# Weight preparation moved from GpSimd to VectorE, and three reorderings, in a retention and two-layer feed-forward kernel

## The chip, the cores and the metric

The kernel runs on one core of a Trainium2 chip. The metric is the device time of one execution in microseconds (us). A core has TensorE (PE, with its weight loads shown as PEld), VectorE (DVE), ScalarE (ACT), GpSimd (POOL) and SyncE (SP, which here issues nearly all DMAs). Each engine runs its own instructions in the order in which they were written; semaphores tie the engines together. Times and rows below come from one profiled execution of the kernel before the change.

## The reference

Inputs are float32. There are 4 batches, 8 heads, 576 positions and a head width of 64, so 2304 tokens of 512 features.

```
scores = (q @ k.T) / sqrt(64)
ret    = scores * gamma_h ** (i - j) for i >= j, else 0
x      = (ret @ v), heads side by side            # 2304 x 512
h = x @ w_in;   g = relu(h) ** 2;              x = g @ w_out     # 512 -> 2048 -> 512
h = x @ w_in2;  g = h * clip(h + 3, 0, 6) / 6; out = g @ w_out2  # 512 -> 2048 -> 512
```

The four weight matrices arrive as 64-bit words and are decoded on the chip to float32.

## The kernel before, in words

Matmuls take float32 operands as a rounded high part and a low part (the rest), and each product is three matmuls: high by high, high by low, low by high (`PASSES`). So every operand has to be split: ACT copies the high part, DVE or POOL subtracts it to get the low part (`split_to`, lines 198 to 206).

The program has three stages. (1) Retention, and the first token block of layer one, up to about 204 us. (2) The rest of layer one, in 48 steps for token blocks of 512 (`units` i = 16 to 63; line 1119). In step i, PE does 12 matmuls for one 128-wide chunk of `h` (line 448) and 12 for the output of the chunk two steps earlier (line 506). ACT then does relu, square and the high copy of g, and the high part of the input weights of step i+2; DVE does the low part of g (line 477) and of those weights (line 201, `win`). (3) Layer two, in three token ranges (`SECOND`). It uses a seven-product scheme for 2 x 2 blocks, in both its matrix products. Each range has a *hidden* part (line 723, 8 pairs of products of `w_in2`) and a *visible* part (line 891: products P1, P2, P6, P5, P7, P3, P4 in `ORDER`, 6 steps each, 12 matmuls in a step).

**Weight preparation for layer two** goes on beside stage 2. `ready_steps` (line 539) makes, for each of 8 pairs of chunks, a list of small jobs with costs. Four are decodes (`dec`: two ACT and four DVE instructions, lines 174 to 194, and one DMA that loads a later weight chunk). One is `sums` (block sums of `w_in2`), with four splits; one is `out_sums` (the same for `w_out2`), with four `out_split`s. Stage 2 hands the jobs out in the 34 steps of `READY` (i = 17 to 58 without the last three and the first of each 16). Each such step earns `pace`, the sum of all costs over 34, and a job is issued once more than half of its cost is owed (lines 1162 to 1167). The costs of a pair sum to 176, so a pair takes 4.25 steps. A split writes a `ready` tile. There are three of these in turn (`bounce`), each is stored to DRAM by a DMA that SP issues (`keep`, line 431, and `keep_right`, line 535), and the store is written only with the next job (`store_late`). A tile is written again only once the store of three splits ago has landed; ACT's high copy is the instruction that waits for that.

**The visible part.** Step s splits the left operand of step s+2 into `gop` tiles: ACT's high copy, then DVE's low part (`split_operand`, line 829). The buffers take turns by three, so ACT's copy waits until PE has done step s-1. For the first `LONE` products these tiles lie in w0 to w2, later in the space of `plain`. After the multiplications of some steps DVE does the block sums of the last three pairs (`sum_up`, line 744), named in the table that `hidden` returns (line 800). The operands of the next range (`operand_items`) and its first weight tiles (`load_left`) are spread over the steps by the table at lines 1202 to 1207. Right operands come by DMA (`load_right`). The first `LONE` x 4 of them, and the four behind, go through four `wo` buffers and are asked for four ahead. Later ones use seven buffers, asked for seven ahead (`ask`, line 899).

**Between stages 2 and 3** the operands of the first range are made (`operand_steps`, line 603), in the order of `PRODUCTS`; the hidden part uses them as P1, P5, P6, P2, P3, P7, (P4).

## Time and profile before

| | |
|---|---|
| median of 3 runs | 856.66 us (856.44 to 857.41) |
| the profiled execution | 856.49 us, of which the span from first to last instruction is 854.7 us |
| PE busy | 823.9 us, 96% |
| PEld busy | 740.2 us, 87% |
| DVE busy | 609.9 us, 71% |
| ACT busy | 495.1 us, 58% |
| POOL busy | 144.4 us, 17% |

PE is busy nearly all the time, but its busy time counts a slowed matmul like any other, so a stage is better judged by comparing the starts of equal groups of matmuls. POOL's work ends with stage 2: after 485 us it does nothing. Up to step i = 17 (about 197 us) the change touches nothing.

### The profile page before, as it was taken

To read this page: it belongs to the slowest core of one execution; us is meant where nothing else is said; L and a number is where in the kernel's file an instruction comes from. 1 tells how busy PE (TensorE), PEld (TensorE's weight loads), DVE (VectorE), ACT (ScalarE), POOL (GpSimd) and SP (SyncE) were. 2 spreads that over 40 slices of the span, in tenths; PEclk is the share of its full clock that TensorE was granted. 3 is DMA by queue.
4 is the path that set the end of the run, shared out by engine and by line. 5 is a ranking of instruction groups with operands and counts; after the bars stand their busy time and mean duration, and the time that the engine had idled before them with its cause. 6 is when DMAs were issued, how large, how long until landed. Compare 5 with 4: busy or idle time off the path is not lost.

```text
span 854.7 us, 14951 instructions
## 1 busy us (share of the span) xinstructions
PE 823.9 (96%) x5580; PEld 740.2 (87%) x5580; DVE 609.9 (71%) x941; ACT 495.1 (58%) x894; POOL 144.4 (17%) x122
## 2 busy tenths in 40 slices
PE   8999999999999999899998999999999999999998
PEld 7888888888777787678876799999999999999998
DVE  5888777786788597794877567687477877476744
ACT  1248676776557676486766444556445455444443
POOL 2362232322344031330421000000000000000000
PEclk9999999999999999999999999999999999999999
DMA  9993665665778768865869477689376697576793
GB/s 361 350 307 125 175 193 179 194 198 196 276 252 290 242 210 300 299 221 188 300 230 330 162 249 255 186 319 402 125 254 230 189 396 283 189 252 201 222 315 122
DMA packets 80609, 208.74 MB, mean 244 GB/s; under 512 B 7958, under 2 KB 29078, under 8 KB 80536
## 3 DMA queue, kind: packets, MB, share of 16 engines
q1 hardware_dynamic: 80244, 207.52, 70.9%
q8 instruction: 44, 0.72, 0.3%
q10 hardware_dynamic: 292, 0.27, 0.1%
q14 instruction: 29, 0.24, 0.1%
HBM read 165.29 MB, written 42.47 MB: 243 GB/s over the span
## 4 chain that ended last, share of the span: by engine, by line
PE 64%; DVE 11%; DMA 10%; ACT 7%; issue 4%; POOL 3%; SPq 1%; ACTq 0%; DVEq 0%; POOLq 0%
PE hps L723 20%; PE yps L891 16%; PE hps L448 12%; PE yps L506 11%; DMA kept<-ready 4%; PE ytail L506 2%; DVE sums L677 2%; DMA stage<-in_w_in_dram 2%; DMA kvt<-in_kv_dram 1%; DVE gop L201 1%; DVE a L188 1%; DVE win L201 1%; ACT r L473 1%; POOL ready L201 1%; DVE g L477 1%
## 5 line engine op out<-in xcount | busy, mean ns | idle before, releaser
L506 PE MATMUL yps<-g,wo 128*128 128x512 f32 x768 | 194.2, 392 | 0.9 <-POOL wo L201 0.9
L448 PE MATMUL hps<-xring,win 128*128 128x512 f32 (+1 forms) x720 | 159.9, 369 | 9.6 <-ACT win L200 5.2
L506 PEld LDWEIGHTS yps<-g,wo 128*128 128x128 f32 x768 | 140.1, 188 | 29.2 <-POOL wo L201 4.1
L448 PEld LDWEIGHTS hps<-xring,win 128*128 128x128 f32 x720 | 124.2, 192 | 36.6 <-DVE win L201 8.6
L891 PE MATMUL yps<-wo,gop 128*128 128x256 f32 x1080 | 134.8, 284 | 3.8 <-DVE gop L201 3.6
L891 PEld LDWEIGHTS yps<-wo,gop 128*128 128x128 f32 x1080 | 131.4, 192 | 6.5 <-DVE gop L201 6.1
L723 PE MATMUL hps<-xlast,win 128*128 128x384 f32 x576 | 108.4, 334 | 0.7 <-DVE xlast L644 0.5
L723 PEld LDWEIGHTS hps<-xlast,win 128*128 128x128 f32 x576 | 100.4, 188 | 1.3 <-DVE xlast L644 0.8
L723 PE MATMUL hps<-xop,win 128*128 128x384 f32 x432 | 82.8, 334 | 0.4 <-ACT xall L766 0.4
L477 DVE TENSOR_TENSOR g<-r,g 128x512 fp32r<-128x512 f32 x64 | 51.0, 797 | 43.9 <-ACT g L474 42.7
L723 PEld LDWEIGHTS hps<-xop,win 128*128 128x128 f32 x432 | 75.5, 188 | 0.8 <-ACT xall L766 0.7
L448 PE MATMUL hps<-xown,win 128*128 128x512 f32 x240 | 62.0, 395 | 6.3 <-DVE win L201 3.5
L470 ACT ACTIVATE r<-hps 128x512 f32<-128x512 f32 x80 | 43.4, 542 | 34.4 <-PE hps L448 34.0
L448 PEld LDWEIGHTS hps<-xown,win 128*128 128x128 f32 x240 | 44.1, 188 | 19.1 <-DVE win L201 6.4
L736 ACT ACTIVATE v<-mixed,half_one 128x768 f32<-128x768 f32 x21 | 19.7, 938 | 61.9 <-DVE mixed L674 61.9
L200 ACT ACTIVATE gop<-sums 128x512 fp32r<-128x512 f32 x54 | 33.4, 629 | 37.8 <-PE yps L891 30.7
L200 ACT ACTIVATE win<-w 128x512 fp32r<-128x512 f32 x64 | 39.7, 620 | 25.3 <-DVE w L194 25.3
L891 PE MATMUL yps<-gop 128*128 128x256 f32 x432 | 53.6, 283 | 0.5 <-ACT xall L944 0.5
L188 DVE SCALAR_TENSOR_TENSOR a<-stage,a 128x512 int32<-128x512 int32 x64 | 51.9, 811 | 1.8
L891 PEld LDWEIGHTS yps<-gop 128*128 128x128 f32 x432 | 52.5, 192 | 0.7 <-ACT xall L944 0.7
L201 DVE TENSOR_TENSOR gop<-sums,gop 128x512 fp32r<-128x512 f32 x54 | 36.4, 689 | 22.3 <-ACT gop L200 22.3
L179 DVE TENSOR_SCALAR a<-a 128x512 f32<-128x512 f32 x64 | 35.6, 557 | 22.5 <-ACT a L175 22.5
(120 smaller groups left out, 1188.6 us busy)
## 6 DMA issues: line engine op xcount, KB each, us to landing
win<-kept SPq DMA_DIRECT2D x72, 512.0 KB
wo<-rights SPq DMA_DIRECT2D x60, 512.0 KB
wo<-kept SPq DMA_DIRECT2D x48, 512.0 KB
stage<-in_w_out_dram SPq DMA_DIRECT2D x32, 512.0 KB
kept<-ready SPq DMA_DIRECT2D x24, 512.0 KB
rights<-ready SPq DMA_DIRECT2D x24, 512.0 KB
gop<-rights SPq DMA_DIRECT2D x24, 512.0 KB
kept<-wo SPq DMA_DIRECT2D x16, 512.0 KB
```

The source lines that it names most:

```text
L179: nc.vector.tensor_scalar(out=a, in0=a, scalar1=LEAST, scalar2=MOST, op0=ALU.max, op1=ALU.min)
L188: nc.vector.scalar_tensor_tensor(out=a.bitcast(I32), in0=high, scalar=-0x40000000, in1=a.bitcast(I32), op0=ALU.bitwise_and, op1=ALU.bitwis ...
L200: lambda: nc.scalar.activation(out=hi, in_=src, func=ACTF.Copy),
L201: lambda: lo_engine.tensor_tensor(out=lo, in0=src, in1=hi.bitcast(F32), op=ALU.subtract),
L448: nc.tensor.matmul(out=h, lhsT=w[:, wp, kk * 128:kk * 128 + 128], rhs=xs[pos, kk][xp][:, o:o + n], start=m == 0, stop=m == 3 * KD - 1,)
L470: relu.append(lambda r=r, h=hs[k]: nc.scalar.activation(out=r, in_=h, func=ACTF.Relu))
L477: low.append(lambda r=r, hi=hi, lo=lo: nc.vector.tensor_tensor(out=lo, in0=r, in1=hi.bitcast(F32), op=ALU.subtract))
L506: nc.tensor.matmul(out=p, lhsT=w[:, wp, m * 128:m * 128 + 128], rhs=g[pos, c][k][:, gpart, :size], start=c == 0 and e == 0 and not (k and ...
L677: nc.vector.tensor_tensor(out=out_, in0=a, in1=b, op=ALU.subtract)
L723: nc.tensor.matmul(out=to, lhsT=w[:, wp, o], rhs=x[:, xp, f], start=first and m == 0, stop=last and m == 5, skip_group_check=True,)
L736: nc.scalar.activation(out=v, in_=src[:, :, p], func=ACTF.Relu, bias=half_one, scale=1.0 / 6.0)
L891: nc.tensor.matmul(out=acc, lhsT=t[:, gp, rows], rhs=w[:, 256 * wp:256 * wp + 256], start=name in ("P1", "P5", "P2") and u in (0, 2) and e ...
```

## The change

It has four parts.

1. `sums` and the low halves of the `w_in2` splits run on DVE where they ran on POOL. Their costs in the list become 17 and 8 (they were 3 and 4), `out_split` costs 8 instead of 9, and a pair's costs sum to 202 (still 4.25 steps).
2. `out_sums` and the four `out_split`s of a pair no longer follow its last job at once. They stand between the next pair's first two decodes and behind the second; those of the last pair still come at the end.
3. The four instructions of each `sum_up` at the start of a visible part are issued one a step, in steps 2 to 13, where they were issued four together in steps 3, 5 and 7. With this `LONE` becomes 3, and the table for the next range's operands and weight tiles starts later (steps 16 to 36 and 19 to 25, which were 9 to 39 and 15 to 21).
4. `PRODUCTS` takes the order of use, and the last four operands of the first range are made ahead of the last two chunks' output copies.

```diff
--- before.py
+++ after.py
@@ -50,7 +50,7 @@
 
 KEPT = ("w0", "w1", "w2", "w3", "w4", "w5", "w6", "x4", "x5", "x6", "xr")
 
-PRODUCTS = ["P1", "P6", "P2", "P7", "P5", "P4", "P3"]
+PRODUCTS = ["P1", "P5", "P6", "P2", "P3", "P7", "P4"]
 
 
 def constants(S, H, D):
@@ -536,6 +536,8 @@
             out=rights[p // 2][:, rows:rows + n, p % 2], in_=t.rearrange("p (a n) -> p a n", a=2)[:, :n].bitcast(F32)
         )
 
+    last_out = []
+
     def ready_steps(p):
         got = {}
 
@@ -551,7 +553,7 @@
             both = place("t6", [128, 2, 512], F32, "sums")
             s0, s1 = both[:, 0], both[:, 1]
             half = lambda t, k: t[:, 256 * k:256 * k + 256]
-            op = nc.gpsimd.tensor_tensor
+            op = nc.vector.tensor_tensor
             op(out=half(s1, 0), in0=half(b, 0), in1=half(b, 1), op=ALU.add)
             op(out=half(s0, 0), in0=half(s1, 0), in1=half(a, 0), op=ALU.subtract)
             op(out=half(s0, 1), in0=half(a, 0), in1=half(b, 0), op=ALU.subtract)
@@ -564,8 +566,10 @@
             t = in_turn("bounce", "t3", 3, [128, 1024], "ready")
             v = t.rearrange("p (a b n) -> p a b n", a=2, b=2)
             only = slice(1, 2) if k == 1 else slice(0, 2)
-            split_to(v[:, only, 0], v[:, only, 1], got["s"][k].rearrange("p (a n) -> p a n", a=2)[:, only], nc.gpsimd)
+            split_to(v[:, only, 0], v[:, only, 1], got["s"][k].rearrange("p (a n) -> p a n", a=2)[:, only], nc.vector)
             late_stores.append(lambda: keep(("s", p, k), t, only))
+
+        c = 2 * p
 
         def out_sums():
             store_late()
@@ -591,11 +595,13 @@
             late_stores.append(lambda: keep_right(p, k, t))
 
         c = 2 * p
-        return [
-            (26, lambda: dec(c, 0)), (26, lambda: dec(c + 1, 0)), (3, sums),
-            (4, lambda: split(0)), (26, lambda: dec(c, 1)), (4, lambda: split(1)), (4, lambda: split(2)),
-            (26, lambda: dec(c + 1, 1)), (4, lambda: split(3)), (17, out_sums),
-        ] + [(9, lambda k=k: out_split(k)) for k in range(4)]
+        before = last_out.copy()
+        last_out[:] = [(17, out_sums)] + [(8, lambda k=k: out_split(k)) for k in range(4)]
+        steps = [(26, lambda: dec(c, 0))] + before[:3] + [(26, lambda: dec(c + 1, 0))] + before[3:] + [
+            (17, sums), (8, lambda: split(0)), (26, lambda: dec(c, 1)), (8, lambda: split(1)), (8, lambda: split(2)),
+            (26, lambda: dec(c + 1, 1)), (8, lambda: split(3)),
+        ]
+        return steps + (last_out if p == NPAIR - 1 else [])
 
 
     operands, lefts, xlast = {}, {}, []
@@ -741,11 +747,17 @@
                 out=to, in0=bent.pop((p, k)), scalar=1.0, in1=to, op0=ALU.min, op1=ALU.mult
             )
 
+        def sum_steps(p):
+            return [
+                lambda: less(sums[:, 1, p], plain[:, 0, p], mixed[:, 1, p]),
+                lambda: add(mixed[:, 1, p], mixed[:, 1, p], mixed[:, 0, p]),
+                lambda: less(sums[:, 0, p], mixed[:, 1, p], plain[:, 0, p]),
+                lambda: less(sums[:, 2, p], plain[:, 1, p], sums[:, 0, p]),
+            ]
+
         def sum_up(p):
-            less(sums[:, 1, p], plain[:, 0, p], mixed[:, 1, p])
-            add(mixed[:, 1, p], mixed[:, 1, p], mixed[:, 0, p])
-            less(sums[:, 0, p], mixed[:, 1, p], plain[:, 0, p])
-            less(sums[:, 2, p], plain[:, 1, p], sums[:, 0, p])
+            for f in sum_steps(p):
+                f()
 
         def fourth(p):
             product(p, "P4", ta[p], False, True)
@@ -797,10 +809,10 @@
             ahead(p, 2)
             add(mixed[:, 0, p], ta[p], p5)
         p = NPAIR - 1
-        return {
-            0: [lambda: bend(p, 1), lambda: close(p, 1)], 1: [lambda: fourth(p), lambda: close(p, 0)],
-            3: [lambda: sum_up(p - 2)], 5: [lambda: sum_up(p - 1)], 7: [lambda: sum_up(p)],
-        }
+        steps = {0: [lambda: bend(p, 1), lambda: close(p, 1)], 1: [lambda: fourth(p), lambda: close(p, 0)]}
+        for i, f in enumerate(sum_steps(p - 2) + sum_steps(p - 1) + sum_steps(p)):
+            steps.setdefault(2 + i, []).append(f)
+        return steps
 
     ORDER = ["P1", "P2", "P6", "P5", "P7", "P3", "P4"]
     NQ = NPAIR // 2
@@ -808,7 +820,7 @@
     FINAL = len(SECOND) - 1
     left_g, right_w = {}, {}
 
-    LONE = 2
+    LONE = 3
     ALONE = LONE * NQ
 
     def load_right(j, s):
@@ -1178,13 +1190,12 @@
                     lows[c - NCH + 3]()
                 if NCH - 4 <= c < NCH - 1:
                     highs[c - NCH + 4]()
+        for i in range(3, 7):
+            highs[i]()
+            lows[i]()
         for u in units[-LAG:]:
             for f in y_steps(*u):
                 f()
-        for i in range(3, 7):
-            highs[i]()
-        for i in range(3, 7):
-            lows[i]()
         for e in (0, 3, 2, 1):
             load_left(1, e)
         early.close()
@@ -1200,11 +1211,11 @@
             side = {}
             if j < FINAL:
                 for i, f in enumerate(operand_items(j + 1)):
-                    side.setdefault(9 + 3 * i, []).append(f)
+                    side.setdefault(16 + 2 * i, []).append(f)
                 k = NPAIR * (j + 1)
                 for i, e in enumerate((0, 3, 2, 1)):
                     side.setdefault(8 + 2 * i, []).append(lambda e=e: load_left(k + 1, e))
-                    side.setdefault(15 + 2 * i, []).append(lambda e=e: load_left(k, e))
+                    side.setdefault(19 + 2 * i, []).append(lambda e=e: load_left(k, e))
             visible(j, side, between)
         while unfinished:
             unfinished.pop(0)()
```

**POOL and DVE, weight preparation.** What POOL has for one pair before; `wd` are decoded weights, `sums` the block sums, `ready` the split tile:

```order
L555 TENSOR_TENSOR sums<-wd 128x256
L556 TENSOR_TENSOR sums<-sums,wd 128x256
L557 TENSOR_TENSOR sums<-wd 128x256
L558 TENSOR_TENSOR sums<-wd,sums 128x256
L201 TENSOR_TENSOR ready<-wd,ready 128x2x256
L201 TENSOR_TENSOR ready<-wd,ready 128x256
L201 TENSOR_TENSOR ready<-sums,ready 128x2x256 x2
```

And the piece of DVE's order, in the changed kernel, that has the first pair's `sums` and first three splits:

```order
L557 TENSOR_TENSOR sums<-wd 128x256
L558 TENSOR_TENSOR sums<-sums,wd 128x256
L559 TENSOR_TENSOR sums<-wd 128x256
L560 TENSOR_TENSOR sums<-wd,sums 128x256
L201 TENSOR_TENSOR ready<-wd,ready 128x2x256
L179 TENSOR_SCALAR a<-a 128x512
L182 TENSOR_SCALAR a<-a 128x512
L188 SCALAR_TENSOR_TENSOR a<-stage,a 128x512
L194 ISA wd<-a,r 128x1024
L477 TENSOR_TENSOR g<-r,g 128x512
L201 TENSOR_TENSOR win<-w_1150,win 128x512
L201 TENSOR_TENSOR ready<-wd,ready 128x256
```

The four sums and the low parts now stand between DVE's decodes (L179 to L194) and its work for PE (`g`, `win`); POOL has none of them.

**DVE, the w_out2 part of the first pair.** Before, `out_sums` and all four `out_split`s together:

```order
L477 TENSOR_TENSOR g<-r,g 128x512
L201 TENSOR_TENSOR win<-w_1317,win 128x512
L577 TENSOR_TENSOR sums<-wd 128x256
L578 TENSOR_TENSOR sums<-wd,sums 128x256
L579 TENSOR_TENSOR sums<-wd 128x256
L580 TENSOR_TENSOR sums<-wd,sums 128x256
L201 TENSOR_TENSOR ready<-wd,ready 128x256
L201 TENSOR_TENSOR ready<-wd,ready 128x2x256
L201 TENSOR_TENSOR ready<-sums,ready 128x2x256
L477 TENSOR_TENSOR g<-r,g 128x512
L201 TENSOR_TENSOR win<-w_1317,win 128x512
L201 TENSOR_TENSOR ready<-sums,ready 128x2x256
```

And now, from the last instruction of `out_sums` (L581 to L584) on:

```order
L584 TENSOR_TENSOR sums<-wd,sums 128x256
L477 TENSOR_TENSOR g<-r,g 128x512
L201 TENSOR_TENSOR win<-w_1317,win 128x512
L201 TENSOR_TENSOR ready<-wd,ready 128x256
L201 TENSOR_TENSOR ready<-wd,ready 128x2x256
L179 TENSOR_SCALAR a<-a 128x512
L182 TENSOR_SCALAR a<-a 128x512
L188 SCALAR_TENSOR_TENSOR a<-stage,a 128x512
L194 ISA wd<-a,r 128x1024
L477 TENSOR_TENSOR g<-r,g 128x512
L201 TENSOR_TENSOR win<-w_1504,win 128x512
L201 TENSOR_TENSOR ready<-sums,ready 128x2x256 x2
```

Two splits follow in the next step, a decode comes between, and the other two stand in the step after that.

**DVE, the start of a visible part.** `gop` is the left operand's low part, L677, L674, L677, L677 one `sum_up`. Before:

```order
L740 SCALAR_TENSOR_TENSOR plain<-xall,plain 128x2x384
L201 TENSOR_TENSOR gop<-plain,gop 128x512 x2
L677 TENSOR_TENSOR sums<-plain,mixed 128x384
L674 TENSOR_TENSOR mixed<-mixed 128x384
L677 TENSOR_TENSOR sums<-mixed,plain 128x384
L677 TENSOR_TENSOR sums<-plain,sums 128x384
L201 TENSOR_TENSOR gop<-plain,gop 128x512 x2
L677 TENSOR_TENSOR sums<-plain,mixed 128x384
L674 TENSOR_TENSOR mixed<-mixed 128x384
```

And now, the same four being L683, L680, L683, L683:

```order
L746 SCALAR_TENSOR_TENSOR plain<-xall,plain 128x2x384
L201 TENSOR_TENSOR gop<-plain,gop 128x512
L683 TENSOR_TENSOR sums<-plain,mixed 128x384
L201 TENSOR_TENSOR gop<-plain,gop 128x512
L680 TENSOR_TENSOR mixed<-mixed 128x384
L201 TENSOR_TENSOR gop<-plain,gop 128x512
L683 TENSOR_TENSOR sums<-mixed,plain 128x384
L201 TENSOR_TENSOR gop<-plain,gop 128x512
L683 TENSOR_TENSOR sums<-plain,sums 128x384
L201 TENSOR_TENSOR gop<-plain,gop 128x512
```

Where two `gop` splits and four sums alternated, one of each does.

## Rows read from the trace of the kernel before

**Rows 1.** Busy time of stage 2: stretch; PE, PEld, DVE, ACT, POOL; clock; DMA.

```profile
203.86:485.32 281.46, 265.70 (x1131) 212.06 (x1129) 211.14 (x310) 185.33 (x331) 77.73 (x64) 0.99 0.73 256
```

**Rows 2.** Timeline of PE in stage 2: start us, us, instruction, count.

```profile
203.86 2.90 PE L448 MATMUL hps<-xown,win 128*128 128x512 f32 x12
...
220.19 2.88 PE L448 MATMUL hps<-xown,win 128*128 128x512 f32 x12
...
477.16 8.32 PE L506 MATMUL yps<-g,wo 128*128 128x512 f32 x36
```

**Rows 3.** Waits of stage 2: engine, line, for whom: us, times, longest.

```profile
ACT ready L200 <- DMA kept<-ready: 48.8, 23, 5.7
...
PEld hps L448 <- DVE win L201: 15.0, 17, 2.1
PEld hps L448 <- ACT win L200: 10.8, 7, 3.0
```

**Rows 4.** DVE's groups in stage 2: shapes, count | busy us, mean ns | idle before.

```profile
L201 DVE TENSOR_TENSOR win<-w,win 128x512 fp32r<-128x512 f32 x44 | 39.9, 906 | 0.0
L477 DVE TENSOR_TENSOR g<-r,g 128x512 fp32r<-128x512 f32 x46 | 37.6, 817 | 36.0 <-ACT g L474 34.8 <-PE yps L506 1.1
L188 DVE SCALAR_TENSOR_TENSOR a<-stage,a 128x512 int32<-128x512 int32 x32 | 29.0, 906 | 1.1
L194 DVE CUSTOM_DVE_ANT_0 wd<-a,r 128x1024 uint16<-128x1024 uint16 x32 | 27.5, 858 | 4.5 <-DVE a L188 0.3 <-ACT r L176 0.2 <-ACT win L200 0.2
L182 DVE TENSOR_SCALAR a<-a 128x512 int32<-128x512 int32 x32 | 20.5, 641 | 1.1
L179 DVE TENSOR_SCALAR a<-a 128x512 f32<-128x512 f32 x32 | 19.9, 622 | 0.8 <-ACT a L175 0.8
L201 DVE TENSOR_TENSOR ready<-sums,ready 128x512 fp32r<-128x512 f32 x16 | 10.9, 690 | 18.1 <-ACT ready L200 18.1
...
L577 DVE TENSOR_TENSOR sums<-wd 128x256 f32<-128x256 f32 x8 | 3.3, 419 | 0.9 <-POOL ready L201 0.9
```

**Rows 5.** The same from 221.9 to 239.9 us, where POOL stands still.

```profile
L194 DVE CUSTOM_DVE_ANT_0 wd<-a,r 128x1024 uint16<-128x1024 uint16 x3 | 2.1, 693 | 0.4 <-DVE a L188 0.2
...
L179 DVE TENSOR_SCALAR a<-a 128x512 f32<-128x512 f32 x3 | 1.3, 421 | 0.0
```

**Rows 6.** Timeline there: a decode's first instruction, and the two behind the decode.

```profile
233.79 0.42 DVE L179 TENSOR_SCALAR a<-a 128x512 f32<-128x512 f32 x1
...
236.15 0.69 DVE L477 TENSOR_TENSOR g<-r,g 128x512 fp32r<-128x512 f32 x1
...
236.75 0.68 DVE L201 TENSOR_TENSOR win<-w,win 128x512 fp32r<-128x512 f32 x1
```

**Rows 7.** Chain of waits: start us, us; two stores from issue to landing.

```profile
245.60 3.04 DMA kept<-ready
...
251.17 8.22 DMA kept<-ready
```

**Rows 8.** Timeline of PE behind stage 2: the first P1, and the first P6.

```profile
485.32 1.22 PE L723 MATMUL hps<-xop,win 128*128 128x384 f32 x6
...
489.16 2.35 PE L723 MATMUL hps<-xop,win 128*128 128x384 f32 x12 [0.36 <-ACT xall L766]
```

**Rows 9.** Chain of waits: undisturbed hidden matmuls, and undisturbed visible ones.

```profile
544.56 2.87 PE yps L891 x24
...
608.31 57.20 PE hps L723 x330
```

**Rows 10.** Timeline of PE, start of the first visible part; waits in brackets.

```profile
555.32 3.13 PE L891 MATMUL yps<-wo,gop 128*128 128x256 f32 x24 [0.56 <-DVE gop L201]
...
562.22 3.98 PE L891 MATMUL yps<-wo,gop 128*128 128x256 f32 x31 [0.31 <-DVE gop L201]
```

**Rows 11.** DMA in a visible part: columns as in Rows 1.

```profile
570.00:574.00 4.00, 4.00 (x36) 4.00 (x35) 2.94 (x4) 2.31 (x4) 0.00 (x0) 1.00 1.03 413
```

**Rows 12.** Chain of waits: a right operand, from issue to landing.

```profile
807.08 6.50 DMA wo<-rights
```

## The prediction

> **What bounds the kernel now.** I read the busy times first. PE is the engine that sets the end (96% of the span), so a microsecond is won only where PE waits, and the question is where it does. To find that I compared the starts of equal groups of matmuls in the timeline of PE. In stage 2 a group of 12 takes 2.72 us undisturbed: 203.86 to 220.19 us is six groups in 16.33 us [rows 2]. From 203.86 us to the first P1 at 485.32 us [rows 2, 8] PE does 46 groups for h (steps 18 to 63) and 48 for y (steps 16 to 63), 94 x 2.72 = 255.7 us of work in 281.5 us. So stage 2 loses 25.8 us. This number has in it the matmuls that run slower after a gap; the granted clock of the stretch is 0.99 [rows 1].
>
> Next I read the waits of that stretch. PE's weight loads wait 15.0 us for DVE's low part of `win` and 10.8 us for ACT's high part [rows 3]. Together that is 25.8 us, the same as the loss, so the split of the next weights, coming late, explains all of it. Neither engine is full on average: 211 us and 185 us of 281 [rows 1]. Why they come late is in two more views.
>
> *DVE.* Its groups take longer on average than the same instructions do while POOL stands still: `win` 0.906 us, L188 0.906, L194 0.858, g 0.817, where a 512-wide instruction with two tensors takes 0.69; L182 0.641 and L179 0.622, where they take 0.42 [rows 4, 5]. (The quiet window gives 0.693 and 0.421 for one of each kind; I use 0.69 and 0.42 for all.) The excess is 44 x 0.216 + 46 x 0.127 + 32 x (0.216 + 0.168 + 0.221 + 0.202) = 9.5 + 5.8 + 25.8 = 41 us, beside 77.7 us of POOL work [rows 1].
>
> *ACT.* It stands 48.8 us, in 23 waits, before a `ready` copy until the store of three splits ago has landed [rows 3]. ACT runs in order, so the relu and the `win` copy behind it are late as well.
>
> **Parts 1 and 2, stage 2.** POOL loses 8 x (4 sums + 4 splits). DVE gains per pair four sums of 0.42, three splits of 0.69 and a half one of 0.42 [rows 4], 4.2 us, or 33 us for 8 pairs. If the excess goes with POOL, DVE is 41 - 33 = 8 us lighter.
>
> Per step: a decode takes DVE 2.36 us, and a 512-wide instruction with another behind it 0.60 us [rows 6]. A pair needs four decodes (9.4), two lots of sums (3.4 at most, 8 x 0.42) and eight splits (6 x 0.60 + 2 x 0.42 = 4.4), 17.2 us in 4.25 steps, or 4.06 us a step; g and `win` add 1.2. That is 5.26 us against PE's 5.44 us. Before, the same sum is 9.4 + 1.7 + 2.2 + 41/8 = 18.4 us a pair, 5.5 us a step: over PE's pace. DVE thus falls from above PE's pace to 97% of it. That is tight, but between the end of one chunk's h and the start of h two steps on PE has three groups (8.2 us), and each 12 steps of preparation are followed by 4 without.
>
> ACT's waits depend on how long after its predecessor's store a tile is asked for again. One unit of cost was worth 5.44/41.4 us (1408 units in 34 steps) and is now worth 5.44/47.5 (1616). Before, the shortest distances were 18 units (the last `out_split`, 2.4 us) and 35 (4.6 us); now they are 42 (4.8 us) and three times 59 (6.8 us), the rest 68 and more. At the end of the list distances down to 16 (1.8 us) remain, and rest steps follow them. A store took 3.0 and 8.2 us to land [rows 7]. With landings spread evenly between these two, an estimate of the waits is (8.2 - d)^2 / (2 x 5.2) for a distance d between them: 1.1 + 3 x 0.2 = 1.7 us a pair, 14 us in all, where there are 48.8. Nor do the stores of `w_in2` wait for POOL any more.
>
> Of PE's 10.8 us behind ACT I keep 10.8 x 14/48.8 = 3.1 us, of its 15.0 us behind DVE 1.2 us (the tight 97%): 4.3 us stay, **21.5 us are won**. The ends are 25.8 us (all), and below nothing, if the excess stays on DVE (third rival).
>
> A rule speaks against this part. The Trainium skill (Perfetto Trace Analysis, Optimizing Scalar/DVE Operations) says that with a saturated DVE it may make sense to move work off to Scalar or even to GpSimd, adding that between DVE and GpSimd this might not help, as they share a port. By its first half the kernel before has the better division, and the sum would be the third rival's 860 us instead of 829; rows 4 and 5 bear out its second half.
>
> **Part 3, the visible parts.** 24 matmuls take 2.87 us undisturbed [rows 9]. From 555.32 to 562.22 us PE does 48 in 6.90 us instead of 5.74, after a gap of 0.56 us, each time until DVE has the low part of `gop` [rows 10]: 1.7 us lost, three times in the kernel, 5.2 us. Before, four sums stood between two pairs of splits. Now DVE has, in a step of 1.44 us (half of 2.87), one split of 0.69 us and one sum of 384 columns (between 0.42 and 0.69; about 0.55), and ACT's copy is done one and a half steps ahead. I take **4.7 us won**, between 0 and 5.2.
>
> What it costs: from step 16 to 36 DVE has 20 splits (13.8 us), 11 items of 768 columns (0.42 and 0.69 for 256 and 512 columns extend to 0.96: 10.6 us) and two additions of results (2.2 us), 26.6 us in 28.8. I take nothing, at most 1 us each in the two ranges that have items. P6's right operands are now asked for four ahead instead of seven, while three and a half weight tiles (1.84 MB) come in at steps 8 to 14. The rights need 0.52 MB in 1.92 us, 273 GB/s, the tiles 160 GB/s; the DMAs moved 413 GB/s at a full share [rows 11]. About 20 GB/s too little for 11.5 us is 0.2 MB, or half a microsecond late, against three tiles' time (5.7 us) to land in; one has taken 6.5 us [rows 12]. I take **0.4 us lost**. The bounds are 0 and the whole 1.84 MB ahead of the rights, 4.5 us, in two ranges: 9 us.
>
> **Part 4, between the stages.** P1 and P5 of the first pair are 12 matmuls, 2.08 us by 57.20 us for 330 [rows 9]; the third product starts after 3.84 us [rows 8]. 1.8 us are lost, because the operands P5 and P6 are split behind P7's and behind the output copies. In order of use, and ahead of these copies, they are ready before PE ends stage 2: 8 ACT and 8 DVE instructions of about 0.55 us in the 8.2 us of the last 36 matmuls. The copies may slip, but only P2's bank waits for one. I take **1.7 us won** (0.7 to 1.8).
>
> **Sum.** 856.5 us (the profiled execution; 1.8 us of it lie outside the span) - 21.5 - 4.7 - 1.7 + 0.4 = 829.0 us. The median of the runs is 0.2 us over the profiled execution. I predict 829 us.
>
> **Rivals.**
> *ACT's waits stay.* The stores take long because loads stand ahead of them, not because they are issued late; the DMA share of 0.73 [rows 1] rises as the stage gets shorter. Then 10.8 us stay, and half of the 15.0, since DVE waits for ACT's copies too (18.1 us before `ready` alone, rows 4). 18.3 us stay instead of 4.3: 843 us. Against it: the new distances.
> *The rights come late.* P6's right operands queue behind the weight tiles: 829 + 9 = 838 us. For it is the 6.5 us of rows 12, against it that the four-ahead stretch before shows waits for `gop` and none for DMA in rows 10.
> *DVE becomes the bound.* If DVE's long durations come from something other than POOL, the excess stays on top of the new work: 5.26 + 41/34 = 6.47 us a step. PE's steps now take 5.44 + 25.8/34 = 6.2 us, so 34 x 0.27 = 9 us are lost, less 6.0 us from parts 3 and 4: 860 us. It is slower than before from about 38 of the 41 us staying. Against it is the quiet window, with 0.693 and 0.421 us [rows 5].
> *The gains are given back*, by DMAs that a faster PE makes late: 856 us.
>
> **Chances.** Forecast 0.72, ACT's waits 0.12, rights 0.07, DVE 0.06, given back 0.03. The forecast's own span is 823.9 (all 32.8 us of loss gone) to 836. The range 823.5 to 841 takes in the rights' case and the better part of the waits' case. A difference under 0.2% can't be told from none here: faster 0.91, same 0.03, slower 0.06.
>
> **What would show it.** Right: in stage 2 DVE's groups at 0.69 and 0.42 us, no POOL, PEld's waits for `win` under 5 us, ACT's waits for stores under 20 us; gaps for `gop` gone; P6 2.1 us behind P1. Wrong: 0.8 us and more for `win` without POOL; ACT's waits above 40 us; new PE waits for `wo<-rights`; or DVE without a pause from step 17 on, with PE behind it.

## The result and the profile after

| | |
|---|---|
| median | 825.4 us (824.7 to 826.54, four runs) |
| the kernel before, same chip | 857.03 us (856.44 to 857.44) |
| ratio | 0.9633 [0.9616, 0.9649] |
| the profiled execution | 825.6 us, span 823.8 us |

The kernel gained 31.6 us; 27.5 us were forecast, and the time lies in the range given. PE is now busy nearly all the time, and POOL has lost 78 us of work. The first part of the page of the kernel after (busy us, share of the span, instructions):

```profile
PE 812.5 (99%) x5580; PEld 740.4 (90%) x5580; DVE 594.5 (72%) x1005; ACT 496.1 (60%) x894; POOL 66.6 (8%) x58
```

**Stage 2.** Its busy times after, in the columns of [rows 1], first from the first group of h to the first P1, then for some ten steps in the middle of it, in which jobs are handed out:

```profile
204.52:460.34 255.82, 255.82 (x1130) 211.64 (x1129) 202.33 (x382) 189.32 (x339) 0.00 (x0) 1.00 0.80 282
286.00:351.00 65.00, 65.00 (x289) 53.81 (x288) 55.58 (x108) 50.02 (x90) 0.00 (x0) 1.00 0.84 296
```

The stage lasts 255.8 us instead of 281.5. That is the 94 x 2.72 = 255.7 us of undisturbed work: nothing is lost any more. DVE has 72 instructions more than before (64 of them POOL's) and is busy 9 us less; the granted clock is 1.00. Its groups (shapes, count | busy us, mean ns | idle before), beside those of [rows 4]:

```profile
L477 DVE TENSOR_TENSOR g<-r,g 128x512 fp32r<-128x512 f32 x46 | 31.7, 689 | 41.1 <-ACT g L474 40.9
L201 DVE TENSOR_TENSOR win<-w,win 128x512 fp32r<-128x512 f32 x44 | 30.1, 684 | 0.0
L194 DVE CUSTOM_DVE_ANT_0 wd<-a,r 128x1024 uint16<-128x1024 uint16 x32 | 22.2, 693 | 4.8 <-ACT r L473 0.5 <-ACT win L200 0.2 <-ACT r L176 0.2
L188 DVE SCALAR_TENSOR_TENSOR a<-stage,a 128x512 int32<-128x512 int32 x32 | 22.2, 692 | 1.1
...
L182 DVE TENSOR_SCALAR a<-a 128x512 int32<-128x512 int32 x32 | 13.7, 427 | 1.1
L179 DVE TENSOR_SCALAR a<-a 128x512 f32<-128x512 f32 x32 | 13.4, 420 | 0.8 <-ACT a L175 0.8
```

Each group has the duration that it had only in the quiet window before [rows 5]. And where DVE stands idle (41.1 us before `g`) it waits for ACT. The waits of the stage (engine, line, for whom: us in total, times, longest), which answer to [rows 3]:

```profile
DVE g L477 <- ACT g L474: 40.9, 22, 4.1
ACT r L470 <- PE hps L448: 36.6, 26, 3.0
ACT ready L200 <- DMA rights<-ready: 17.9, 16, 3.5
...
ACT ready L200 <- DMA kept<-ready: 3.4, 4, 1.1
...
PEld hps L448 <- DVE win L201: 0.2, 1, 0.2
```

The row of PEld behind ACT's `win` is gone, the one behind DVE's is down from 15.0 to 0.2 us. ACT still waits 21.3 us for stores (55.3 us before, in two rows: the 48.8 of [rows 3] and 6.5 for `rights`), but PE sees none of it. The 36.6 us that ACT waits for PE's `hps` say that ACT is now ahead of PE.

**Between the stages and in the visible part.** The timeline of PE after, at the end of stage 2, and in the first visible part (start us, us, instruction, count):

```profile
452.18 8.32 PE L506 MATMUL yps<-g,wo 128*128 128x512 f32 x36
460.34 3.31 PE L729 MATMUL hps<-xop,win 128*128 128x384 f32 x18
463.49 3.28 PE L729 MATMUL hps<-xlast,win 128*128 128x384 f32 x18
...
521.48 26.80 PE L903 MATMUL yps<-wo,gop 128*128 128x256 f32 x218
```

The first three products take 3.15 us and the fourth starts without a gap; before, the third came 3.84 us after the first instead of 2.08 [rows 8]. The first visible part runs in one piece, 218 matmuls up to the end of the window shown, where [rows 10] had gaps for `gop`. In the second visible part there is something new. Its timeline (the bracket: idle time before, and who ended it):

```profile
649.77 12.36 PE L903 MATMUL yps<-wo,gop 128*128 128x256 f32 x101
663.03 2.41 PE L903 MATMUL yps<-wo,gop 128*128 128x256 f32 x18 [0.90 <-DMA wo<-rights]
665.67 2.50 PE L903 MATMUL yps<-wo,gop 128*128 128x256 f32 x19 [0.22 <-DMA wo<-rights]
```

PE waits for right operands; before, its weight loads did so once, for 0.3 us. The chain of waits there shows what it waited for, a transfer from issue to landing (start us, us):

```profile
657.77 7.77 DMA wo<-rights
```

### The profile page after: what moved, and what is told of

The parts are those of the page before. It is cut to its first block, busy times and chain, and to the rows that moved or that the text cites. A ratio compares the mean times of both kernels' runs of the same rounds, so it can differ in the third digit from the quotient of the medians.

```text
span 823.8 us, 14936 instructions
## 1 busy us (share of the span) xinstructions
PE 812.5 (99%) x5580; PEld 740.4 (90%) x5580; DVE 594.5 (72%) x1005; ACT 496.1 (60%) x894; POOL 66.6 (8%) x58
## 4 chain that ended last, share of the span: by engine, by line
PE 88%; DMA 6%; SPq 2%; issue 1%; DVE 1%; ACT 0%; POOL 0%; ACTq 0%; POOLq 0%; DVEq 0%
PE hps L448 22%; PE yps L903 21%; PE hps L729 21%; PE yps L506 21%; PE ytail L506 3%; DMA kvt<-in_kv_dram 2%; DMA qkt<-in_qk_dram 1%; DMA wo<-rights 1%; DMA early<-in_qk_dram 1%; DMA stage<-in_w_in_dram 1%; DMA early<-in_kv_dram 1%; SPq L1010 0%; DMA stage<-in_w_out_dram 0%; SPq L279 0%; POOL win L201 0%
## 5 line engine op out<-in xcount | busy, mean ns | idle before, releaser
L448 PE MATMUL hps<-xring,win 128*128 128x512 f32 (+1 forms) x720 | 153.5, 362 | 0.1
L903 PE MATMUL yps<-wo,gop 128*128 128x256 f32 x1188 | 146.5, 284 | 1.7 <-DMA wo<-rights 1.1
L903 PEld LDWEIGHTS yps<-wo,gop 128*128 128x128 f32 x1188 | 144.1, 192 | 3.3 <-DMA wo<-rights 1.3
L448 PEld LDWEIGHTS hps<-xring,win 128*128 128x128 f32 x720 | 123.0, 189 | 21.5 <-ACT r L470 0.3
L477 DVE TENSOR_TENSOR g<-r,g 128x512 fp32r<-128x512 f32 x64 | 45.1, 705 | 49.1 <-ACT g L474 48.8
L448 PE MATMUL hps<-xown,win 128*128 128x512 f32 x240 | 59.6, 389 | 0.0
L473 ACT ACTIVATE r<-r 128x512 f32<-128x512 f32 x80 | 47.2, 590 | 2.5
L188 DVE SCALAR_TENSOR_TENSOR a<-stage,a 128x512 int32<-128x512 int32 x64 | 45.0, 704 | 1.8
L175 ACT ACTIVATE a<-stage 128x512 f32<-128x512 f32 x64 | 42.3, 661 | 5.9 <-DMA stage<-in_w_in_dram 5.9
L179 DVE TENSOR_SCALAR a<-a 128x512 f32<-128x512 f32 x64 | 29.2, 456 | 22.6 <-ACT a L175 22.6
```

The costliest lines, as they stand in the source:

```text
L175: nc.scalar.activation(out=a, in_=high.bitcast(F32), func=ACTF.Abs)
L179: nc.vector.tensor_scalar(out=a, in0=a, scalar1=LEAST, scalar2=MOST, op0=ALU.max, op1=ALU.min)
L188: nc.vector.scalar_tensor_tensor(out=a.bitcast(I32), in0=high, scalar=-0x40000000, in1=a.bitcast(I32), op0=ALU.bitwise_and, op1=ALU.bitwis ...
L448: nc.tensor.matmul(out=h, lhsT=w[:, wp, kk * 128:kk * 128 + 128], rhs=xs[pos, kk][xp][:, o:o + n], start=m == 0, stop=m == 3 * KD - 1,)
L473: nc.scalar.activation(out=r, in_=r, func=ACTF.Square)
L477: low.append(lambda r=r, hi=hi, lo=lo: nc.vector.tensor_tensor(out=lo, in0=r, in1=hi.bitcast(F32), op=ALU.subtract))
```

## The experiments

My theory was that of the prediction: in stage 2 two separate causes, POOL lengthening DVE's instructions (15.0 us of PE's waits) and ACT stopped by stores (10.8 us). The main rivals: that the two are one thing, so that either part alone does it; that DVE's long durations do not come from POOL; and that DVE at 97% is what decides. Stage 2 below is the time from the first group of step 18 to the first P1, 281.46 us before and 255.82 after; the rest is what follows it up to the end of the last matmul, 366.0 us before and 360.1 after. By the profiles, 25.6 us of the gain lie in stage 2 and 5.9 us behind it. (Ahead of it the profile after is 0.7 us longer; with stage 2 unchanged, in the runs of parts 3 and 4, it begins 1.2 and 1.6 us later than before, so that is no effect of the change.)

**Each part alone, on the kernel before.** Part 1 alone, with the old order of the jobs:

```diff
-            op = nc.gpsimd.tensor_tensor
+            op = nc.vector.tensor_tensor
...
-            split_to(v[:, only, 0], v[:, only, 1], got["s"][k].rearrange("p (a n) -> p a n", a=2)[:, only], nc.gpsimd)
+            split_to(v[:, only, 0], v[:, only, 1], got["s"][k].rearrange("p (a n) -> p a n", a=2)[:, only], nc.vector)
...
-            (26, lambda: dec(c, 0)), (26, lambda: dec(c + 1, 0)), (3, sums),
-            (4, lambda: split(0)), (26, lambda: dec(c, 1)), (4, lambda: split(1)), (4, lambda: split(2)),
-            (26, lambda: dec(c + 1, 1)), (4, lambda: split(3)), (17, out_sums),
-        ] + [(9, lambda k=k: out_split(k)) for k in range(4)]
+            (26, lambda: dec(c, 0)), (26, lambda: dec(c + 1, 0)), (17, sums),
+            (8, lambda: split(0)), (26, lambda: dec(c, 1)), (8, lambda: split(1)), (8, lambda: split(2)),
+            (26, lambda: dec(c + 1, 1)), (8, lambda: split(3)), (17, out_sums),
+        ] + [(8, lambda k=k: out_split(k)) for k in range(4)]
```

> Part 1 alone on the kernel before: the w_in2 sums and splits on DVE, w_out2's jobs still in one lump. Theory (two separate causes, as the prediction has it: POOL's work lengthens DVE's instructions, 15.0 us of PE's waits; late stores hold ACT, 10.8 us): DVE's groups at 0.69 and 0.42 us, the 15.0 us gone, ACT's waits for stores little changed (about 47 us by the distances of 16 and 33 cost units), so 857 - 15 = 842 us. Rival (POOL is behind both, since its late low parts also make the stores late): ACT's waits fall below 25 us by part 1 alone and the whole 25.8 us come back: 831 us.

850.8 us (848.53 to 851.71), ratio 0.9928 [0.9911, 0.9946]; stage 2 takes 273.53 us, 7.9 us less than before. Its waits in that stage:

```profile
ACT ready L200 <- DMA kept<-ready: 36.0, 14, 4.9
...
PEld hps L448 <- ACT win L200: 12.0, 5, 4.9
...
ACT ready L200 <- DMA rights<-ready: 8.1, 5, 2.2
PEld hps L448 <- DVE win L201: 4.4, 10, 0.6
```

Without POOL every group of DVE has its short duration (L188 0.693, `win` 0.685 us), and PE's wait for DVE falls from 15.0 to 4.4 us. But ACT still stands 44.1 us before stores (55.3 before), and PE 12.0 us behind it. Neither expected time came.

Part 2 alone, with POOL and its costs as before:

```diff
-        return [
-            (26, lambda: dec(c, 0)), (26, lambda: dec(c + 1, 0)), (3, sums),
...
-        ] + [(9, lambda k=k: out_split(k)) for k in range(4)]
+        before = last_out.copy()
+        last_out[:] = [(17, out_sums)] + [(9, lambda k=k: out_split(k)) for k in range(4)]
+        steps = [(26, lambda: dec(c, 0))] + before[:3] + [(26, lambda: dec(c + 1, 0))] + before[3:] + [
...
+        return steps + (last_out if p == NPAIR - 1 else [])
```

> Part 2 alone on the kernel before: w_out2's jobs between the next pair's decodes, POOL keeps its work. Theory (two separate causes): DVE's long durations stay (excess about 41 us), ACT's waits fall to about 15 us and with them 7 of its 10.8 us: 850 us. Rival one (distances between stores are everything): 835 us or less. Rival two (POOL is behind both): waits for stores of w_in2 stay, 855 to 857 us.

841.39 us (839.93 to 842.85), ratio 0.9815 [0.9796, 0.9835]; stage 2 takes 263.58 us, 17.9 us less. Its waits there:

```profile
ACT ready L200 <- DMA rights<-ready: 21.9, 18, 2.6
PEld hps L448 <- DVE win L201: 7.8, 7, 2.2
ACT ready L200 <- DMA kept<-ready: 7.1, 5, 2.5
...
PEld hps L448 <- ACT win L200: 1.2, 2, 0.6
```

None of the three expected times came. DVE's instructions are still long here (`win` 0.829, L188 0.880 us), and yet PE's wait for DVE is halved. That DVE can pass ACT's stops on under its own name is shown by the run with two `ready` tiles below: with POOL idle, longer stops of ACT alone bring 6.5 us of waits for DVE's `win`. But part 2 also takes apart DVE's own lump, `out_sums` and four `out_split`s in a row, and no run separates the lump from the spacing of the stores. So the two causes are neither one nor apart in the shares that I had given them. In the profiled executions the effects add up: 7.9 + 17.9 = 25.8 us, and both parts together gave 25.6.

Part 3 alone (`sum_steps` one a step, `LONE` and the table as in the changed kernel):

```diff
-            3: [lambda: sum_up(p - 2)], 5: [lambda: sum_up(p - 1)], 7: [lambda: sum_up(p)],
+        for i, f in enumerate(sum_steps(p - 2) + sum_steps(p - 1) + sum_steps(p)):
+            steps.setdefault(2 + i, []).append(f)
...
-    LONE = 2
+    LONE = 3
...
-                    side.setdefault(9 + 3 * i, []).append(f)
+                    side.setdefault(16 + 2 * i, []).append(f)
...
-                    side.setdefault(15 + 2 * i, []).append(lambda e=e: load_left(k, e))
+                    side.setdefault(19 + 2 * i, []).append(lambda e=e: load_left(k, e))
```

> Part 3 alone on the kernel before (border sums one a step, LONE 3, later items). Theory: the waits for gop in the three visible parts go (5.2 us), and up to 1.3 us come back as waits for right operands where weight tiles are loaded at steps 8 to 14: 852 to 853 us; stage 2 stays at 281 us. Rival (the gaps for gop are covered by something else that is late, such as the right operands): 856 us or more.

853.84 us (852.55 to 856.85), ratio 0.9953 [0.9933, 0.9973]: about the theory's time. Stage 2 is unchanged (281.35 us), the rest 3.7 us shorter. All of PE's gaps for `gop` at the start of the visible parts are gone; in their place are four for rights. Two of them in its timeline of PE:

```profile
568.73 4.88 PE L897 MATMUL yps<-wo,gop 128*128 128x256 f32 x36 [0.20 <-DMA wo<-rights]
573.84 2.39 PE L897 MATMUL yps<-wo,gop 128*128 128x256 f32 x18 [0.23 <-DMA wo<-rights]
```

Part 4 alone:

```diff
-PRODUCTS = ["P1", "P6", "P2", "P7", "P5", "P4", "P3"]
+PRODUCTS = ["P1", "P5", "P6", "P2", "P3", "P7", "P4"]
...
+        for i in range(3, 7):
+            highs[i]()
+            lows[i]()
         for u in units[-LAG:]:
             for f in y_steps(*u):
                 f()
-        for i in range(3, 7):
-            highs[i]()
-        for i in range(3, 7):
-            lows[i]()
```

> Part 4 alone on the kernel before (order of the first range's operands). Theory: P6 starts 2.1 us behind P1 instead of 3.8: 1.8 us less, 855.4 us. Rival (the output copies, now behind the operands, are late for P2's bank): 857 us, no difference, with a new wait of PE some 3 us behind P1.

856.2 us (854.84 to 859.46), ratio 0.9984 [0.9968, 1.0]: by the times alone hardly to be told from no change. The timeline of PE in this kernel shows the step itself:

```profile
486.74 3.31 PE L723 MATMUL hps<-xop,win 128*128 128x384 f32 x18
489.88 3.28 PE L723 MATMUL hps<-xlast,win 128*128 128x384 f32 x18
```

The first product's 18 matmuls and the second's run in one piece, and the rest of the program is 2.0 us shorter.

By the medians of all runs the four parts alone are worth 6.5, 16.0, 4.1 and 1.7 us, each with an interval of some 1.5 us either way. That is 28.3 of the 31.6 us; whether the last 3 us come only with the parts together, these runs do not tell.

**Is it POOL that lengthens DVE?** The changed kernel, with two subtractions on POOL that nobody needs in `sums` and in each `split`:

```diff
+            nc.gpsimd.tensor_tensor(out=cst[:, :256], in0=cst[:, 256:512], in1=cst[:, 512:768], op=ALU.subtract)
```

> The changed kernel with idle work for POOL: ten subtractions of 256 columns a pair, on constants that nothing reads any more, 80 instructions or about 80 us. Nothing waits for them. Theory (POOL's reading lengthens DVE's instructions, whatever else hangs on POOL): excess of 30 to 45 us on DVE again, 5.26 + 41/34 = 6.47 us a step, stage 2 longer by up to 35 us: 845 to 860 us. Rival (POOL did harm as a link in the chain, by late results and stores): 825 us, no change.

856.24 us (854.62 to 858.12), ratio 0.9986 [0.9974, 0.9998]: the whole gain is gone. POOL's 80 instructions have no data that anyone uses and wait for nobody; they run back to back from 198.6 to 279.2 us. Groups on POOL and DVE from 205 to 279 us, beside these reads:

```profile
L543 POOL TENSOR_TENSOR cst<-cst 128x256 f32<-128x256 f32 x73 | 69.0, 945 | 5.7
L201 DVE TENSOR_TENSOR win<-w,win 128x512 fp32r<-128x512 f32 x8 | 9.7, 1218 | 0.0
L188 DVE SCALAR_TENSOR_TENSOR a<-stage,a 128x512 int32<-128x512 int32 x8 | 8.9, 1107 | 0.3
...
L182 DVE TENSOR_SCALAR a<-a 128x512 int32<-128x512 int32 x9 | 7.6, 843 | 0.3
```

The same from 285 to 491 us, when POOL has stopped:

```profile
L201 DVE TENSOR_TENSOR win<-w,win 128x512 fp32r<-128x512 f32 x36 | 24.6, 685 | 0.0
...
L188 DVE SCALAR_TENSOR_TENSOR a<-stage,a 128x512 int32<-128x512 int32 x23 | 15.9, 693 | 0.8
L182 DVE TENSOR_SCALAR a<-a 128x512 int32<-128x512 int32 x23 | 9.8, 427 | 0.8
```

Beside the reads these three take 1.6 to 2 times as long, and behind them they are as short as in the kernel after.

PE's timeline has five gaps for DVE's `win`, 19.0 us in all, the last up to 282.3 us:

```profile
227.46 4.63 PE L448 MATMUL hps<-xown,win 128*128 128x512 f32 x10 [5.22 <-DVE win L201]
...
246.70 3.96 PE L448 MATMUL hps<-xown,win 128*128 128x512 f32 x10 [5.17 <-DVE win L201]
```

The matmuls behind the gaps are slower as well. The granted clock is 1.00 up to 216 us, 0.64 from 227 to 235 us, right behind the first gap of 5.2 us (a mean of its two levels, 1.2 and 2.4 GHz), and 0.88 over 205 to 282 us. The stage is 30.1 us longer than after; the profiled execution is the longest of the ten.

Here the reads stand in one piece, and DVE, busy 97% from 205 to 282 us, has no time to catch up. Spread out as in the kernel before, POOL's work costs less: 7.9 us by part 1 alone, and 7.8 us by part 2 alone set beside the kernel after (263.58 and 255.82 us).

The same kernel with four fills on POOL in each of these places, which write and read nothing:

```diff
+            nc.gpsimd.memset(cst[:, :512], 0.0)
```

> The same with 160 POOL memsets of 512 columns in the place of the subtractions: POOL writes and reads nothing. Theory (POOL and DVE collide where both read): DVE's groups stay at 0.69 and 0.42 us, 825 us. Rival (any POOL instruction lengthens DVE's): excess as in the run with subtractions, in proportion to POOL's busy time, 840 us and more.

828.21 us (827.57 to 829.11), ratio 0.9662 [0.9646, 0.9678], nearer to the theory than to the rival. Its groups in stage 2:

```profile
L543 POOL MEMSET cst<- 128x512 f32 x150 | 83.5, 556 | 8.6
L477 DVE TENSOR_TENSOR g<-r,g 128x512 fp32r<-128x512 f32 x46 | 31.7, 689 | 34.3 <-ACT g L474 34.2
L201 DVE TENSOR_TENSOR win<-w,win 128x512 fp32r<-128x512 f32 x44 | 30.1, 684 | 0.0
L188 DVE SCALAR_TENSOR_TENSOR a<-stage,a 128x512 int32<-128x512 int32 x32 | 22.2, 693 | 1.1
...
L182 DVE TENSOR_SCALAR a<-a 128x512 int32<-128x512 int32 x32 | 17.3, 542 | 1.1
L179 DVE TENSOR_SCALAR a<-a 128x512 f32<-128x512 f32 x32 | 14.4, 449 | 0.8 <-ACT a L175 0.8
```

POOL is no less busy than with the subtractions, without a pause from 198.0 to 295.9 us, and DVE's instructions with two tensors do not feel it. Only those with one tensor and a scalar grow. The stage is 2.9 us longer. So it is what POOL reads that lengthens the instructions with two tensors. This is as the Trainium skill has it (SBUF — State Buffer, Who interferes with whom): a DVE instruction with two inputs in SBUF contends with a GpSimd instruction that reads SBUF and not with one that only writes, while a `tensor_scalar` can enter a mode that takes the port pair which DVE shares with GpSimd. The trace agrees: `win` is at 0.684 us beside the fills, and L182 at 0.542 us where it takes 0.427 alone.

**How much room has DVE?** The changed kernel, with one more DVE instruction of 256 columns in each `split` and `out_split`, 64 in all:

```diff
+        nc.vector.tensor_tensor(out=cst[:, :256], in0=cst[:, 256:512], in1=cst[:, 512:768], op=ALU.min)
```

> The changed kernel with one more DVE subtraction-like instruction (256 columns, on constants that nothing reads) with each of the 64 splits: 64 x 0.42 us, 0.66 us a step more by starts. Theory (the prediction's sum: DVE needs 5.26 of PE's 5.44 us in a step): 5.9 us a step, stage 2 longer by 34 x 0.48 = 16 us: 841 us. Rival (DVE has more room than that sum says, as its busy share of 86% in these steps suggests; 4.7 + 0.66 = 5.4 us): 826 to 828 us.

831.59 us (830.24 to 832.06), ratio 0.9686 [0.9662, 0.971]; stage 2 is 6.0 us longer than after, between theory and rival. Its busy time from 204 to 266 us (columns of [rows 1]):

```profile
204.00:266.00 62.00, 62.00 (x276) 51.43 (x275) 58.55 (x120) 46.84 (x85) 0.00 (x0) 1.00 0.83 293
```

With DVE busy 94% of these 62 us PE doesn't wait at all. PE's waits for `win` in the whole stage (us in total, times, longest):

```profile
PEld hps L448 <- ACT win L200: 2.6, 1, 2.6
PEld hps L448 <- DVE win L201: 2.4, 3, 1.3
```

An instruction of 256 columns with another behind it takes 0.34 us (by the starts in DVE's timeline), so DVE got 64 x 0.34 = 22 us more. PE's weight loads wait 2.4 us for it in the stage, and 2.6 us for ACT, where they waited 0.2 us for both in the kernel after: DVE had room for most of this work, but not for all.

**What do ACT's store waits need?** The changed kernel with two `ready` tiles in turn instead of three:

```diff
-            t = in_turn("bounce", "t3", 3, [128, 1024], "ready")
+            t = in_turn("bounce", "t3", 2, [128, 1024], "ready")
```

> The changed kernel with two ready tiles in turn in the place of three. The distances fall to 25 to 51 cost units (2.9 to 5.8 us), ACT's waits for stores rise from 21 us to 60 to 90 us by the prediction's estimate. Theory (what counts is the sum: ACT needs about 4.3 us of a step, and only 1.1 us a step, 39 us in all, can be waited without PE): 845 us and more, with PE waiting for ACT's win copies. Rival (each wait for itself counts, and none of under 5 us reaches PE): 825 to 830 us.

847.83 us (847.42 to 853.89), ratio 0.9909 [0.9876, 0.9942]; stage 2 of the profiled execution, the longest of these runs, takes 281.68 us. Its waits there:

```profile
ACT ready L200 <- DMA rights<-ready: 35.2, 16, 5.3
...
ACT ready L200 <- DMA kept<-ready: 21.4, 11, 3.1
PEld hps L448 <- ACT win L200: 15.5, 7, 3.4
```

The time is as the theory had it, though the waits for stores came to 56.6 us and not to 60 to 90. The stores alone, with POOL idle, can cost most of the gain (22 of 31 us by the medians). Set beside the other kernels this gives a picture of when ACT's stops reach PE (all in us, in stage 2 of the profiled executions):

| kernel | ACT waits for stores | PEld waits for ACT's `win` | PEld waits for DVE's `win` | stage 2 beyond 255.7 |
|---|---|---|---|---|
| after | 21.3 | none | 0.2 | 0.1 |
| extra DVE work | 28.5 | 2.6 | 2.4 | 6.1 |
| part 2 alone | 29.0 | 1.2 | 7.8 | 7.9 |
| POOL reads | 31.0 | none | 22.3 | 30.2 |
| POOL fills | 33.1 | none | 3.5 | 3.0 |
| part 1 alone | 44.1 | 12.0 | 4.4 | 17.8 |
| before | 55.3 | 10.8 | 15.0 | 25.8 |
| two tiles | 56.6 | 15.5 | 6.5 | 26.0 |

Up to some 33 us in the stage nearly all of it is hidden; from 44 us a fifth to over a quarter reaches PE. The total does not decide alone (55.3 us cost less than 44.1), and stops close to each other seem to cost more. In part 1 alone one stop of 4.3 us, at 228 us, is followed by no gap of PE. Four stops of 1.2 to 3.1 us between 248 and 257 us are followed by one of 1.6 us; the last of them, and the gap:

```profile
256.59 0.63 ACT L200 ACTIVATE ready<-sums 128x512 fp32r<-128x512 f32 x1 [1.26 <-DMA rights<-ready]
...
260.72 1.57 PE L448 MATMUL hps<-xown,win 128*128 128x512 f32 x4 [1.59 <-ACT win L200]
```

This fits a lead of ACT that the stops use up; how long the lead is was not measured.

**Who makes the rights late?** The changed kernel with the four weight loads of steps 8 to 14 (three whole tiles and a half one) moved to steps 27 to 33:

```diff
-                    side.setdefault(8 + 2 * i, []).append(lambda e=e: load_left(k + 1, e))
+                    side.setdefault(27 + 2 * i, []).append(lambda e=e: load_left(k + 1, e))
```

> The changed kernel with the weight tiles of the next range's second pair loaded at steps 27 to 33 of a visible part, which were loaded at 8 to 14. Theory (the right operands of P6 queue behind these tiles): the wait for wo<-rights at 662 us (0.9 + 0.2 us) goes, 1.3 us less than the changed kernel: 824.1 us. Rival (the right operands are late by themselves, asked for four ahead): the wait stays, 825.4 us.

824.08 us (823.52 to 824.49). The same again, with the changed kernel on the same chip:

> The changed kernel with the second pair's weight tiles at steps 27 to 33, against the changed kernel on the same chip. Theory (those tiles hold up the right operands, about 2 us from the first P1 on): 1.5 to 2.5 us less. Rival (the 1.3 us between the two in other calls was the chip): no difference beyond 0.5 us.

> The changed kernel once more, on one chip with the next one, so that the two can be compared: 825 to 826 us.

823.77 us (823.7 to 824.51) against 825.84 us (824.66 to 827.1): 2.1 us less, and the ranges don't overlap. PE's timeline of the second run, at the place of the two gaps:

```profile
641.08 32.13 PE L903 MATMUL yps<-wo,gop 128*128 128x256 f32 x264
```

No gap: these weight loads were what made the rights late. Whether the rights stood behind them in a queue or shared the bandwidth with them was not separated. This version is faster than both kernels of the change.

## Why the prediction was right, and where it was off

- **Where the loss was.** Right. 25.8 us were lost in stage 2 by the spacing of PE's groups, and 25.6 came back.
- **POOL makes DVE's instructions long.** Right. They are at 0.69 and 0.42 us without it (after, and part 1 alone), and long again with POOL's reads (the idle subtractions). With that the rival "DVE becomes the bound", 860 us, is out. The rule that the prediction weighed would have had the kernel before as the better one; here taking work off GpSimd for DVE won 7.9 us by itself, and 81 us of POOL's reads in one piece cost 30 us.
- **15.0 us to DVE and 10.8 us to ACT.** Wrong as shares. A wait names the engine that came last, and DVE can come last because ACT stopped it, or because its own jobs stand in a lump. Part 1 alone won 7.9 us and part 2 alone 17.9. By the medians part 1 came out 9 us above its forecast (850.8 against 842) and part 2 9 us below (841.4 against 850). The prediction made one sum of both parts, where the two errors, of opposite sign, cancel: the time that came says nothing for the shares, and in that respect the hit is luck.
- **The term that was mis-sized: "4.3 us stay".** Only 0.1 us stayed. For ACT, I expected 14 us of store waits and scaled PE's 10.8 us with them, 3.1 us. The waits were 21.3 us, half as much again and just over the 20 that I had set as a sign, and still cost PE nothing: the scaling with the total was wrong, since waits of up to 33 us hardly reach PE (the table above). For DVE, the 1.2 us for "the tight 97%" had no ground either: from 286 to 351 us after, DVE is busy 86%, and with 22 us more work the wait for DVE is 2.4 us. One reason is that the need was put too high; the four sums take 1.48 us, not 1.7 (233.71 to 235.19 us in the timeline of DVE after). How the rest divides between that and the lead of 8.2 us that the prediction names was not measured.
- **Part 3.** All of the 5.2 us came back where I took 4.7. The 0.4 us for the rights were 1.1 us by the spacing (5.2 + 1.8 gained, 5.9 seen behind stage 2), 1.5 us with part 3 alone, and about 2 us by the version without it: three to five times as large, between the bounds of 0 and 9 us. Here the working was wrong. A right operand serves 18 matmuls (the x18 above), which is 2.15 us and not 1.92, so the rights need 244 GB/s and the tiles 160, together less than the 413 of [rows 11]: by that sum nothing would have come late. It did, and moving the weight loads ended it, so a balance of mean rates was the wrong measure. The rival "the rights come late" happened, in small, and with it one of the signs that I had named for being wrong.
- **Part 4.** 1.7 us predicted; 1.8 us by the spacing of the products, 2.0 us by the rest of the program with part 4 alone.
- **The sum.** The profiled executions differ by 856.5 - 825.6 = 30.9 us: 25.6 in stage 2 and 5.9 behind it, less 0.7 ahead of it. Of the 3.4 us that the forecast lay above the profiled execution, 4.1 came from stage 2 (25.6 against 21.5); behind it the errors cancel (5.9 against 6.0), and 0.7 lies ahead of it.

Open: why the rights took 7.77 us to land at 657.77 us. From 650 to 660 us the DMA share is 0.84 at 283 GB/s, below the 413 GB/s of a full share [rows 11]; what each transfer waited for in the queues was not tried.

## What to carry to other kernels

When two waits name two engines on one chain, don't give each cause its own microseconds from the list of waits: take each cause away alone, because an engine that runs in order passes its stop on under its own name. Don't scale the cost of a wait with its total either: here store waits of up to 33 us cost PE almost nothing, so ask first how far ahead the engine runs. And before moving two-tensor work to POOL, look at DVE's mean durations in a window with POOL and in one without: an idle-looking engine can be taking the time of the busy one.

## What the runs showed of the hardware

- POOL's reads lengthen DVE's instructions: beside subtractions on POOL without a pause, from 0.69 to between 0.99 and 1.22 us for 512 columns with two tensors, from 0.42 to 0.95 us for 256 columns, and from 0.42 to between 0.84 and 0.90 us for one tensor and a scalar (POOL reads, 205 to 279 us). DVE's two copies of `yps`, whose source lies in PSUM, stayed at 0.68 us in that stretch.
- POOL's fills leave the instructions with two tensors as they are (0.684 to 0.693 us), although they lengthen the int32 form of an instruction with one tensor and a scalar from 0.427 to 0.542 us in the mean of the stage, and the f32 form only from 0.420 to 0.449. That the two forms differ so much I had not expected.
- A transfer of 512 KB took 3.0 us from issue to landing in one place (a store, [rows 7]) and 7.8 us in another (a load, after). Where the weight tiles beside the latter were moved away, PE no longer waited for it.
